# First-batch scans with one operand in PSUM, and a layer norm split between ScalarE and VectorE

## The chip, the cores and the metric

The kernel runs on one core of a Trainium2 chip. The metric is the device time of one execution in microseconds (us), lower is better; it is measured three times and the median is compared. The engines have short names here, as in the profile: PE is TensorE (its matmuls), PEld its weight loads, DVE is VectorE, ACT is ScalarE, POOL is GpSimd, and SP issues the transfers. Each engine takes its own instructions strictly in order and waits at an instruction whose inputs are not there, while whatever stands behind it waits too.

## The reference, cut to what matters

Three layers follow one another. The first is a recurrent attention with a decay for each key channel, the second a gated block with a layer norm, the third a gated convolution:

```python
state = np.zeros((B, H, D, D))                          # B = 4, H = 8, D = 48, S = 768
for t in range(S):
    cur = einsum('bhd,bhe->bhde', u * kt, vt)
    y[:, :, t] = einsum('bhd,bhde->bhe', rt, state + cur)
    state = wt[..., None] * state + einsum('bhd,bhe->bhde', kt, vt)

h = gelu(x @ w_in)                                      # x is y with the heads side by side
u, v = h[..., :512], h[..., 512:]
v_n = (v - mean(v)) / sqrt(var(v) + 1e-6) * g_ln        # the layer norm
gated = u * (einsum('ts,bsd->btd', w_sg, v_n) + b_sg)
x = x + gated @ w_out

gate = sigmoid(causal_conv5(x))
return (gate * (x @ w_val)) @ w_out2
```

## The kernel before

The attention is cut into 48 units: 4 batches, 3 segments of 256 tokens, 4 pairs of heads. Inside a unit the recurrence is done in 4 chunks of 64 tokens. `suffix` (step F, L270) multiplies the decays from the end of each chunk backwards by one scan on DVE; `prefix` (step E, L275) does it forwards. A scan is one instruction in which each column needs the result of the column before it; it reads two operands, `data0` and `data1`. For F and E the first is the decays `w` out of the loaded packet `pk`, and the second is a row of zeros with one entry for each chunk, where the product starts anew: `D1F` for F, `D1E` for E, both in SBUF. `r_part` and `k_part` (L, K) scale the queries and keys on POOL, `turn` (t) transposes the keys on PE, `scores` (s) and `causal` (m) make the masked products inside a chunk, and `kv` (B, L323) makes the sum of key-value products of each chunk in PSUM tile `a1`. `kv_out` (d, L346) copies them on ACT into the SBUF tile `SD1`, whose column 1 of every 6 holds the state that `keep` (p) carried over from the segment before. `states` (a, L350) then runs the third scan over 288 columns, `SD1` with `SD0` (the decays of whole chunks, put there by `chunk_decay`, D, on ACT), in place. `s_part` (S) copies the states on ACT, `tokens` (C, L366) makes the outputs on PE in another PSUM tile, `a2`, and `y_out` (y) adds them to `y` on DVE. In the first batch odd units have their PSUM tiles in another pool (`c0`, `c1`, `c2`).

In the first batch `warm` (L319) puts 3 extra bf16 matmuls of 256 columns ahead of `kv` and 2 ahead of `tokens`; their results are never read. Before, they are written into the tile that the real matmuls use afterwards, so they wait until that tile is free. 16 wider ones stand at the start of the program (L703, tile `wps`).

After the attention come, for each 128 tokens, a transpose (`xT`, L482 on DVE), `hv` (L490 and on: the matmul with the v half of `w_in`, gelu, layer norm and a split of the result in a high and a low part, so that three fp32r matmuls give an fp32 product), and for each half batch `u_step`, `vs_step` (the product with `w_sg`, tile `vps`), `gated`, `wo_step`, `conv`, `val_step`, `out_step`. Weights arrive as 64-bit numbers and are turned into fp32 by one ACT and four DVE instructions each (`to_f32`, L150 to L157), then split on ACT and POOL (L163, L164). The steps of batch b+1's attention are interleaved with the later layers of batch b by hand-written lists (`ORDER0`, `ORDER`, `LAST`), and within these a list scheduler with a priority table (`LEAD`) orders each engine's instructions by its own model of time.

Of the kernel before, what the change touches and what calls it, by code (L numbers as in the profile page):

```python
# [52 lines left out]
def tile_kernel(ctx, tc, pk, sv_, rk_, v_, u_, misc_, w_in, w_sgT, b_sg, w_o1, w_val,  # L53
# [193 lines left out]
    def unit(n):  # L247
# [22 lines left out]
        def suffix():  # L270
            dve.tensor_tensor_scan(out=F[:, NW:0:-1], data0=w[:, NW:0:-1], data1=D1F[:, NW:0:-1],  # L271
                                   initial=0.0, op0=ALU.mult, op1=ALU.add)
            dve.reciprocal(out=d1e[:, 0:NW:W1], in_=F[:, 1:NW + 1:W1])

        def prefix():  # L275
            dve.tensor_tensor_scan(out=E, data0=w[:, 0:NW], data1=d1e, initial=0.0,
                                   op0=ALU.mult, op1=ALU.add)
# [41 lines left out]
        def warm(o, k):  # L319
            for _ in range(k if first else 0):  # L320
                pe.matmul(out=o[:, 256:512], lhsT=wsrc[:, 0:128], rhs=wsrc[:, 0:256], start=True, stop=True)

        def kv():  # L323
            t["b"] = ps(1, n, [128, 512])
            warm(t["b"], WB)
            for j in range(NT):
                for hh in range(2):
                    pe.matmul(out=t["b"][half[hh], 2 * j * D:(2 * j + 2) * D],  # L328
                              lhsT=kn[:, j * 128 + 64 * hh:j * 128 + 64 * hh + 64],
                              rhs=vcd[:, j, :, hh * D:(hh + 1) * D], start=True, stop=True)  # L330
            if summed:
                for j in range(NT):
                    pe.matmul(out=t["b"][:, NC * D + 2 * j:NC * D + 2 * j + 2],
                              lhsT=q[:, j * 128:(j + 1) * 128], rhs=u_col[:, 2 * p:2 * p + 2], start=True, stop=True)

        def own_v():
            rs = r2.tile([128, 2 * NT], F32, tag="rsw", name="rsw")
            act.activation(out=rs, in_=t["b"][:, NC * D:NC * D + 2 * NT], func=AF.Copy)
# [49 lines left out]

# [450 lines left out]
```

## Time and profile before

| | us |
|---|---|
| median of 3 runs (lowest, highest) | 556.61 (556.54, 557.25) |
| the profiled execution | 556.39 |
| span of its instructions in the trace | 554.3 |
| PE / DVE / ACT / POOL busy in that span | 520.3 / 417.0 / 296.2 / 267.5 |

The span runs from the first instruction to the last; 2.1 us of the profiled execution lie around it. Busy time is the union of an engine's instructions. [...]

### The profile page before, as it was taken

The numbers are of one execution on the slowest core, as the hardware profiler recorded it, in microseconds if no ns is written. First come the engines' busy times: TensorE is split into PE (matmuls) and PEld (weight loads), VectorE is DVE, ScalarE is ACT, GpSimd is POOL, SyncE is SP. The second block draws the span as 40 slices with busy tenths as digits, with TensorE's granted clock in tenths as the row PEclk, the third lists the DMA queues.
The fourth block names the chain that finished last, engine by engine and source line by source line (L and its number), as shares of the span: only waits on it lengthen the run. The fifth ranks groups of instructions, "written<-read, shape, count | busy, mean of one in ns | idle before, by whom it ended". The sixth has DMA issues, their size and how long they took to land.

```text
span 554.3 us, 10705 instructions
## 1 busy us (share of the span) xinstructions
PE 520.3 (94%) x4060; PEld 448.4 (81%) x4060; DVE 417.0 (75%) x823; ACT 296.2 (53%) x695; POOL 267.5 (48%) x282
## 2 busy tenths in 40 slices
PE   8978688979999999898999999999999999999995
PEld 4666566868988887787988888789989887999985
DVE  6999999899697769985299669965498349324673
ACT  4676856655475745743285746643484636323233
POOL 7477856674844246764154126861163125523430
PEclk9598788896999999999999999999999999999999
DMA  8961513424314343342115342232122100100002
GB/s 302 388 246 44 164 66 103 133 83 158 86 43 138 108 144 100 100 128 90 41 38 178 124 122 72 59 121 80 44 54 91 58 16 1 43 1 0 1 0 86
DMA packets 27075, 53.42 MB, mean 96 GB/s; under 512 B 3089, under 2 KB 17169, under 8 KB 27025
## 3 DMA queue, kind: packets, MB, share of 16 engines
q1 hardware_dynamic: 27024, 52.75, 29.4%
q8 instruction: 32, 0.52, 0.4%
q14 instruction: 19, 0.15, 0.1%
HBM read 48.02 MB, written 4.72 MB: 95 GB/s over the span
## 4 chain that ended last, share of the span: by engine, by line
PE 40%; DVE 16%; issue 3%; DMA 2%; POOL 1%; ACT 1%; POOLq 0%; SPq 0%; ACTq 0%; DVEq 0%
PE vps L522 12%; PE c L586 6%; PE ups L522 6%; PE o L644 4%; DVE cvp L618 4%; PE val L522 3%; PE a L372 3%; PE hv L499 2%; PE a L303 2%; PE a L328 2%; DVE cv L618 1%; PE a L297 1%; DVE SD L353 1%; DVE rk L229 1%; DMA rk<-in_rk_dram 1%
## 5 line engine op out<-in xcount | busy, mean ns | idle before, releaser
L522 PE MATMUL vps<-wsg,vnt 128*128 128x384 f32 x576 | 113.1, 341 | 0.0
L522 PEld LDWEIGHTS vps<-wsg,vnt 128*128 128x128 f32 x576 | 101.1, 190 | 1.0
L573 POOL TENSOR_TENSOR gt<-gt,ut 128x384 f32<-128x384 f32 x32 | 33.8, 1057 | 98.7 <-DVE gt L562 80.5
L499 PE MATMUL hv<-win,x 128*128 128x512 f32 x216 | 65.2, 431 | 3.7 <-DVE cv L631 2.2
L586 PE MATMUL c<-gl,late 128*128 128x384 f32 x288 | 62.6, 345 | 0.0
L522 PE MATMUL ups<-x,win 128*128 128x384 f32 x288 | 59.8, 350 | 1.5 <-DVE gt L562 1.5
L358 ACT ACTIVATE SE<-SD 64x192 f32<-64x192 f32 x80 | 45.1, 564 | 23.1 <-DVE SD L353 13.9
L522 PEld LDWEIGHTS ups<-x,win 128*128 128x128 f32 x288 | 51.4, 192 | 3.0 <-DVE gt L562 1.9
L586 PEld LDWEIGHTS c<-gl,late 128*128 128x128 f32 x288 | 50.2, 189 | 2.2
L499 PEld LDWEIGHTS hv<-win,x 128*128 128x128 f32 x216 | 41.4, 202 | 12.8 <-DVE cv L631 2.6
L280 POOL TENSOR_TENSOR L<-pk,E 128x256 f32<-128x256 f32 x38 | 30.9, 814 | 41.1 <-PE a L372 32.9
L618 DVE SCALAR_TENSOR_TENSOR cvp<-x,cw_col,cvp 128x384 f32<-128x384 f32 x84 | 48.7, 612 | 0.4 <-ACT cvp L615 0.2
L271 DVE TENSOR_TENSOR_SCAN F<-pk,D1F 128x260 f32<-128x260 f32 x40 | 35.3, 884 | 16.5 <-DMA pk<-in_pk_dram 12.3
L353 DVE TENSOR_TENSOR_SCAN SD<-SD,SD 128x288 f32<-128x288 f32 x48 | 43.4, 903 | 4.6 <-ACT SD L347 4.2
L522 PE MATMUL val<-x2hl,late 128*128 128x384 f32 x216 | 44.2, 344 | 2.2 <-ACT vg L503 1.8
L644 PE MATMUL o<-late,ml 128*128 128x384 f32 x216 | 43.9, 342 | 0.7 <-DVE ml L634 0.7
L316 ACT ACTIVATE vcd<-v 64x192 f32<-64x192 f32 x84 | 30.2, 359 | 26.8 <-PE a L328 25.8
L515 POOL TENSOR_TENSOR vnt<-vg,vnt 128x512 fp32r<-128x512 f32 x24 | 34.2, 1426 | 17.9 <-ACT vnt L514 15.3
L576 DVE TENSOR_TENSOR gl<-gt,gl 128x384 fp32r<-128x384 f32 x32 | 20.0, 624 | 29.9 <-ACT gl L575 29.7
L522 PEld LDWEIGHTS val<-x2hl,late 128*128 128x128 f32 x216 | 37.3, 188 | 5.3 <-ACT vg L503 2.7
L575 ACT ACTIVATE gl<-gt 128x384 fp32r<-128x384 f32 x32 | 16.7, 523 | 42.9 <-POOL gt L573 38.2
L644 PEld LDWEIGHTS o<-late,ml 128*128 128x128 f32 x216 | 37.5, 187 | 2.4 <-DVE ml L634 1.0
(154 smaller groups left out, 1102.8 us busy)
## 6 DMA issues: line engine op xcount, KB each, us to landing
pk<-in_pk_dram SPq DMA_DIRECT2D x40, 386.5 KB, 3.4
sv<-in_sv_dram SPq DMA_DIRECT2D x39, 192.0 KB, 2.4
v<-in_v_dram SPq DMA_DIRECT2D x12, 384.0 KB, 3.3
out_dram<-ot SPq DMA_DIRECT2D x24, 192.0 KB, 1.9
rk<-in_rk_dram SPq DMA_DIRECT2D x12, 384.0 KB, 3.1
bits<-in_w_in_dram SPq DMA_DIRECT2D x6, 512.0 KB, 6.8
room_l<-in_pk_dram SPq DMA_DIRECT2D x7, 386.5 KB, 7.1
bits<-in_w_o_dram SPq DMA_DIRECT2D x7, 384.0 KB, 5.3
```

Source lines behind the costliest of these rows:

```text
L271: dve.tensor_tensor_scan(out=F[:, NW:0:-1], data0=w[:, NW:0:-1], data1=D1F[:, NW:0:-1], initial=0.0, op0=ALU.mult, op1=ALU.add)
L280: pool.tensor_tensor(out=ch(L[:, 0, :]), in0=ch(r), in1=e3[:, :, 0:C], op=ALU.mult)
L316: act.activation(out=vcd[half[c2], :, c2, :], in_=vt[b, s][half[c2], :, 2 * p * D:(2 * p + 2) * D], func=AF.Copy)
L353: dve.tensor_tensor_scan(out=SD1, data0=SD1, data1=SD0, initial=0.0, op0=ALU.add, op1=ALU.mult)
L358: act.activation(out=S[half[hh], :, hh, :], func=AF.Copy, in_=d1[half[hh], :, 1:NC + 1].rearrange("p e c -> p c e"))
L499: pe.matmul(out=ps, lhsT=x[:, a, kk, j * 128:(j + 1) * 128], rhs=win[:, w, kk, DV:2 * DV], start=(z == 0), stop=(z == nmm - 1))
L515: pool.tensor_tensor(out=vnt[b][:, 1, i, :], in0=vg, in1=hi.bitcast(F32), op=ALU.subtract)]
L522: pe.matmul(out=ps, lhsT=lhs(a, kk), rhs=rhs(w, kk), start=(z == 0), stop=(z == nk * 3 - 1))
L573: pool.tensor_tensor(out=t, in0=t, in1=ut.pop((b, hf, d)), op=ALU.mult)
L586: pe.matmul(out=acc[0][f], lhsT=late["wo1"][:, a, d, f * 128:(f + 1) * 128], rhs=g[:, w, :], start=(d == 0 and q == 0), stop=(d == KV - 1 ...
L618: dve.scalar_tensor_tensor(out=t, in0=x2[:, f, k:k + HALF], scalar=cw_col[:, f, k:k + 1], in1=t, op0=ALU.mult, op1=ALU.add)
L644: pe.matmul(out=acc2[0][j], lhsT=m[:, a, j * 128:(j + 1) * 128], rhs=late["wo2"][:, w, g, :], start=(g == 0 and q == 0), stop=(g == KD - 1 ...
```

## The change

There are two edits in one.

In the first batch all three scans get one operand in PSUM. A PSUM tile `D1` (a whole bank, the one that was `a2`) holds the start entries of both F and E. `kv` writes its products with a stride of 6 columns straight to where the third scan reads them, so the copy `kv_out` goes; the carried state comes into the same tile by an ACT copy of two columns of every 6 (a DVE memset in the first segment), and `keep` goes. `tokens` writes into the rest of the same bank, which is therefore held until `y_out`. The extra matmuls no longer write to the tile of the real ones but to `wps`, which is kept for that.

The layer norm's `(v - mean) * rstd` was one DVE instruction. Now ACT makes `mean - v` and the high part (`* rstd` on the way), and DVE makes the low part in one instruction with two SBUF inputs, which was POOL's. The sign is put right by a negated `g_ln` (`g_neg`).

```diff
-        F, E, d1e = buf("F", n), buf("E", n), buf("D1E", n)
+        F, E = buf("F", n), buf("E", n)
+        d1e, d1f = (D1, D1[:, D1F0:]) if first else (buf("D1E", n), D1F)
+        kvs = lambda: t["b"][:, 0:SDN].rearrange("p (e c) -> p e c", c=NC + 2)
+        KV0 = SDN + TOK if first else NC * D
...
-            dve.tensor_tensor_scan(out=F[:, NW:0:-1], data0=w[:, NW:0:-1], data1=D1F[:, NW:0:-1],
+            dve.tensor_tensor_scan(out=F[:, NW:0:-1], data0=w[:, NW:0:-1], data1=d1f[:, NW:0:-1],
...
-        def warm(o, k):
+        def warm(k):
             for _ in range(k if first else 0):
-                pe.matmul(out=o[:, 256:512], lhsT=wsrc[:, 0:128], rhs=wsrc[:, 0:256], start=True, stop=True)
+                pe.matmul(out=wps[:, 0:256], lhsT=wsrc[:, 0:128], rhs=wsrc[:, 0:256], start=True, stop=True)
...
-                    pe.matmul(out=t["b"][half[hh], 2 * j * D:(2 * j + 2) * D],
-                              lhsT=kn[:, j * 128 + 64 * hh:j * 128 + 64 * hh + 64],
+                    o = (kvs()[half[hh], :, 2 + 2 * j:4 + 2 * j].rearrange("p e c -> p c e") if first
+                         else t["b"][half[hh], 2 * j * D:(2 * j + 2) * D])
+                    pe.matmul(out=o, lhsT=kn[:, j * 128 + 64 * hh:j * 128 + 64 * hh + 64],
                               rhs=vcd[:, j, :, hh * D:(hh + 1) * D], start=True, stop=True)
...
         def kv_out():
+            if first:
+
+                if s == 0:
+                    dve.memset(kvs()[:, :, 0:2], 0.0)
+                else:
+                    act.activation(out=kvs()[:, :, 0:2], in_=d1[:, :, NC:NC + 2], func=AF.Copy)
+                return
             act.activation(out=d1[:, :, 2:NC + 2], func=AF.Copy,
...
-            dve.tensor_tensor_scan(out=SD1, data0=SD1, data1=SD0, initial=0.0,
+            dve.tensor_tensor_scan(out=SD1, data0=t["b"][:, 0:SDN] if first else SD1, data1=SD0, initial=0.0,
                                    op0=ALU.add, op1=ALU.mult)
...
-            if s < NSEG - 1:
+            if s < NSEG - 1 and not first:
                 act.activation(out=d1[:, :, 1], in_=d1[:, :, NC + 1], func=AF.Copy)
...
-            t["c"] = ps(2, n, [128, 512])
-            warm(t["c"], WC)
+            t["c"] = t["b"][:, SDN:SDN + TOK] if first else ps(2, n, [128, 512])[:, 0:TOK]
+            warm(WC)
...
-            ln = dve.tensor_scalar(out=vg, in0=vg, scalar1=mv[:, 0:1], scalar2=rs,
-                                   op0=ALU.subtract, op1=ALU.mult)
+
+            ln = act.activation(out=vg, in_=vg, func=AF.Identity, scale=-1.0, bias=mv[:, 0:1])
             hi = vnt[b][:, 0, i, :]
-            last[b * KS + i] = [ln, act.activation(out=hi, in_=vg, func=AF.Copy),
-                       pool.tensor_tensor(out=vnt[b][:, 1, i, :], in0=vg, in1=hi.bitcast(F32),
-                                          op=ALU.subtract)]
+            last[b * KS + i] = [ln, act.activation(out=hi, in_=vg, func=AF.Copy, scale=rs),
+                       dve.scalar_tensor_tensor(out=vnt[b][:, 1, i, :], in0=vg, scalar=rs,
+                                                in1=hi.bitcast(F32), op0=ALU.mult, op1=ALU.subtract)]
...
+    dve.memset(D1, 0.0)
+    dve.memset(D1[:, D1F0 + W1:D1F0 + NW + 1:W1], 1.0)
...
-    wps = psD.tile([128, 512], F32, tag="d", name="wps")
+    wps = psC.tile([128, 512], F32, tag="c2", name="wps")
```

The scheduler orders the instructions anew. On PE, at the start of the program, the kernel before has ten of the narrow extra matmuls (L321, into the tiles of the real ones) behind the 16 wide ones, and then the transposes and products of units 0 and 1. These rows run from the last extra matmul to the first unit's products (`a_204` and `a_224` are PSUM tiles of unit 0, `a_241` and `a_279` of unit 1, `kh` the scaled keys, `kn` their transpose):

```order
L321 LDWEIGHTS D1F
L321 MATMUL a_279<-D1F 128x256
L297 MATMUL a_204<-ident,kh_106 128x128 x2
L297 MATMUL a_241<-ident,kh_107 128x128 x2
L303 MATMUL a_204<-L_101,kh_106 64x64 x8
L328 MATMUL a_224<-vcd_119,kn_111 64x96 x4
L333 MATMUL a_224<-misc,pk_99 128x2 x2
```

In the changed kernel, on PE at the same place, eleven narrow extra matmuls stand ahead of the first transpose, one between the two transposes, and 21 behind them (the last pair of these rows is the first of the 21):

```order
L306 MATMUL a_208<-ident,kh_108 128x128 x2
L330 LDWEIGHTS D1F
L330 MATMUL wps<-D1F 128x256
L306 MATMUL a_245<-ident,kh_109 128x128 x2
L330 LDWEIGHTS D1F
L330 MATMUL wps<-D1F 128x256
```

So 33 extra matmuls now run ahead of the first unit's scores where ten did; 16 more stand between the transposes of units 2 and 3, 6 behind these, and the last of all 60 is issued ahead of unit 3's `kv`.

On DVE, the rows of the kernel before from the third unit's E scan to the second unit's masking (scans are listed here under the name SCALAR_TENSOR_TENSOR; L276 is the scan E, L271 F, L353 the scan over the states, L311 the masking, L291 the product of queries and keys):

```order
L276 SCALAR_TENSOR_TENSOR E_110<-room_l,D1E_112 128x260
L271 SCALAR_TENSOR_TENSOR F_109<-room_l,D1F 128x260
L291 TENSOR_TENSOR room_l<-room_l 128x256
L311 TENSOR_TENSOR L_101<-a_204,misc 128x256
L273 RECIPROCAL D1E_112<-F_109 128x4
L276 SCALAR_TENSOR_TENSOR room_w<-room_l,D1E_112 128x260
L353 SCALAR_TENSOR_TENSOR SD_115<-SD_115,SD_113 128x288
L311 TENSOR_TENSOR L_102<-a_241,misc 128x256
```

In the changed kernel, on DVE, the rows from the fourth unit's E scan on (L285 is that scan, `D_96` the PSUM tile `D1`, L157 to L163 the weights' conversion, L320 the masking, L360 the new memset in unit 0's PSUM tile):

```order
L285 SCALAR_TENSOR_TENSOR room_w<-room_l,D_96 128x260
L300 TENSOR_TENSOR room_l<-room_l 128x256
L157 TENSOR_SCALAR spare<-spare 128x512
L159 TENSOR_SCALAR spare<-spare 128x512
L161 SCALAR_TENSOR_TENSOR spare<-bits,spare 128x512
L157 TENSOR_SCALAR spare<-spare 128x512
L320 TENSOR_TENSOR L_103<-a_208,misc 128x256
L163 SCALAR_TENSOR_TENSOR spare<-bits,spare 128x512
L159 TENSOR_SCALAR spare<-spare 128x512
L360 MEMSET a_228 128x48x2
L320 TENSOR_TENSOR L_104<-a_245,misc 128x256
```

The maskings have moved behind all four units' F and E scans and behind four instructions of the weights' conversion, and the first scan over the states comes later still.

## Rows read from the trace of the kernel before

**Rows 1.** The page's head: span; busy time, share and instructions of the engines.

```profile
span 554.3 us, 10705 instructions
PE 520.3 (94%) x4060; PEld 448.4 (81%) x4060; DVE 417.0 (75%) x823; ACT 296.2 (53%) x695; POOL 267.5 (48%) x282
```

**Rows 2.** Windows: stretch, length, busy of each engine (instructions), granted clock, DMA share, GB/s.

```profile
10.00:74.70 64.70, 52.78 (x533) 39.77 (x534) 62.79 (x106) 44.54 (x116) 47.29 (x46) 0.78 0.59 212
...
84.20:141.00 56.80, 50.95 (x378) 42.61 (x378) 52.50 (x109) 32.91 (x80) 33.25 (x33) 0.85 0.38 118
141.00:520.00 379.00, 371.95 (x2890) 329.83 (x2889) 268.96 (x541) 198.48 (x457) 168.55 (x173) 1.00 0.25 76
```

**Rows 3.** Windows of L271 (scan F) alone, DVE, the first batch's twelve.

```profile
0.00:74.70 74.70, 11.79 (x12) 0.81 0.62 219
```

**Rows 4.** Windows of L276 (scan E) alone, DVE, the first batch's twelve.

```profile
0.00:74.70 74.70, 11.97 (x12) 0.81 0.62 219
```

**Rows 5.** Windows of L353 (scan over the states) alone, DVE, the first batch's twelve.

```profile
0.00:84.20 84.20, 10.85 (x12) 0.82 0.56 199
```

**Rows 6.** Instructions of one line: shortest/median/longest ns, first and last start (us).

```profile
L271 DVE TENSOR_TENSOR_SCAN F<-room_l,D1F x7: 668/700/1696, 9.8 to 64.5; 128x260 f32<-128x260 f32 x7
L276 DVE TENSOR_TENSOR_SCAN E<-room_l,D1E x4: 685/844/997, 10.8 to 49.6; 128x260 f32<-128x260 f32 x4
L353 DVE TENSOR_TENSOR_SCAN SD<-SD,SD x12: 717/945/1181, 14.7 to 83.1; 128x288 f32<-128x288 f32 x12
L311 DVE TENSOR_TENSOR L<-a,misc x42: 374/411/425, 13.1 to 441.4; 128x256 f32<-128x256 f32 x42
L283 DVE TENSOR_TENSOR kh<-pk,F x36: 390/426/1248, 75.6 to 427.1; 128x256 f32<-128x256 f32 x36
```

**Rows 7.** Timeline of DVE and POOL: start, duration (us), engine, line, operation.

```profile
3.83 0.70 DVE L271 TENSOR_TENSOR_SCAN F<-pk,D1F 128x260 f32<-128x260 f32 x1 [1.47 <-DMA pk<-in_pk_dram]
...
13.09 0.41 DVE L311 TENSOR_TENSOR L<-a,misc 128x256 f32<-128x256 f32 x1
...
30.27 1.70 DVE L271 TENSOR_TENSOR_SCAN F<-room_l,D1F 128x260 f32<-128x260 f32 x1
...
30.01 1.40 POOL L164 TENSOR_TENSOR win<-spare,win 128x512 fp32r<-128x512 f32 x1 [0.68 <-ACT win L163]
```

**Rows 8.** Timeline of PE: start, duration (us), line, operation.

```profile
7.02 1.04 PE L321 MATMUL a<-D1F 128*128 128x256 bf16 x8
...
9.92 0.68 PE L303 MATMUL a<-L,kh 64*64 64x64 f32 x16 [1.26 <-ACT kn L307]
10.53 0.55 PE L328 MATMUL a<-vcd,kn 128*64 128x96 f32 x8
```

**Rows 9.** Groups by line, whole span: count, busy us, mean ns, idle before.

```profile
L155 DVE SCALAR_TENSOR_TENSOR spare<-bits,spare 128x512 int32<-128x512 int32 x6 | 5.1, 848 | 0.1
L157 DVE SCALAR_TENSOR_TENSOR spare<-bits,spare 128x512 int32<-128x512 int32 x6 | 4.5, 743 | 0.0
L352 DVE MEMSET SD<- 128x48 f32 x16 | 1.6, 98 | 3.4 <-ACT SE L358 1.8 <-DMA pk<-in_pk_dram 1.0 <-POOL SD L697 0.7
L347 ACT ACTIVATE SD<-a 128x192 f32<-128x192 f32 x48 | 16.1, 336 | 6.0 <-PE a L328 3.2 <-PE a L333 2.0
L514 ACT ACTIVATE vnt<-vg 128x512 fp32r<-128x512 f32 x24 | 15.1, 630 | 28.7 <-DVE vg L511 26.6 <-DVE rstd L509 1.8 <-DVE x L544 0.2
L515 POOL TENSOR_TENSOR vnt<-vg,vnt 128x512 fp32r<-128x512 f32 x24 | 34.2, 1426 | 17.9 <-ACT vnt L514 15.3 <-DMA pk<-in_pk_dram 2.5
```

**Rows 10.** Windows of L511 (the layer norm's DVE instruction) alone, up to 141 us.

```profile
0.00:141.00 141.00, 4.44 (x6) 0.83 0.49 166
```

**Rows 11.** Windows of L321 (the extra matmuls) alone: PE, PEld, clock.

```profile
40.00:84.20 44.20, 5.11 (x25) 2.45 (x25) 0.81 0.27 86
```

**Rows 12.** Windows, all engines, columns as in group 2.

```profile
12.00:24.00 12.00, 11.16 (x97) 8.27 (x95) 10.54 (x22) 8.55 (x24) 6.82 (x8) 0.51 1.04 392
40.00:76.00 36.00, 27.91 (x249) 20.69 (x246) 35.69 (x61) 25.67 (x64) 28.45 (x27) 0.78 0.29 94
```

More of the change, by code (lines that the diff above doesn't have):

```diff
@@ L74, in tile_kernel @@
     u_bc = const.tile([128, DM], F32, name="u_bc")
+    g_neg = const.tile([128, KV], F32, name="g_neg")
     b_bc = const.tile([128, S], F32, name="b_bc")
@@ L78, in tile_kernel @@
     D1F = const.tile([128, NW + 1], F32, name="D1F")
+    D1 = psA.tile([128, 512], F32, tag="a2", name="D1")
+    D1F0 = NW - W1
     SDN = D * (NC + 2)
@@ L270, in suffix @@
         def suffix():
-            dve.tensor_tensor_scan(out=F[:, NW:0:-1], data0=w[:, NW:0:-1], data1=D1F[:, NW:0:-1],
+            dve.tensor_tensor_scan(out=F[:, NW:0:-1], data0=w[:, NW:0:-1], data1=d1f[:, NW:0:-1],
                                    initial=0.0, op0=ALU.mult, op1=ALU.add)
-            dve.reciprocal(out=d1e[:, 0:NW:W1], in_=F[:, 1:NW + 1:W1])
+            dve.reciprocal(out=d1e[:, 0:NW - C:W1], in_=F[:, 1:NW + 1:W1])
         def prefix():
-            dve.tensor_tensor_scan(out=E, data0=w[:, 0:NW], data1=d1e, initial=0.0,
+            dve.tensor_tensor_scan(out=E, data0=w[:, 0:NW], data1=d1e[:, 0:NW], initial=0.0,
                                    op0=ALU.mult, op1=ALU.add)
@@ L332, in kv @@
                 for j in range(NT):
-                    pe.matmul(out=t["b"][:, NC * D + 2 * j:NC * D + 2 * j + 2],
+                    pe.matmul(out=t["b"][:, KV0 + 2 * j:KV0 + 2 * j + 2],
                               lhsT=q[:, j * 128:(j + 1) * 128], rhs=u_col[:, 2 * p:2 * p + 2], start=True, stop=True)
@@ L337, in own_v @@
             rs = r2.tile([128, 2 * NT], F32, tag="rsw", name="rsw")
-            act.activation(out=rs, in_=t["b"][:, NC * D:NC * D + 2 * NT], func=AF.Copy)
+            act.activation(out=rs, in_=t["b"][:, KV0:KV0 + 2 * NT], func=AF.Copy)
             if p == 0:
@@ L350, in states @@
         def states():
-            if s == 0:
+            if s == 0 and not first:
                 dve.memset(d1[:, :, 1], 0.0)
-            dve.tensor_tensor_scan(out=SD1, data0=SD1, data1=SD0, initial=0.0,
+            dve.tensor_tensor_scan(out=SD1, data0=t["b"][:, 0:SDN] if first else SD1, data1=SD0, initial=0.0,
                                    op0=ALU.add, op1=ALU.mult)
@@ L376, in y_out @@
             y = yt[b, s][:, :, 2 * p * D:(2 * p + 2) * D]
-            dve.tensor_tensor(out=y, in0=t["c"][:, 0:NT * 2 * D].rearrange("p (j e) -> p j e", j=NT), in1=y, op=ALU.add)
+            dve.tensor_tensor(out=y, in0=t["c"].rearrange("p (j e) -> p j e", j=NT), in1=y, op=ALU.add)
         steps = {"F": suffix, "E": prefix, "L": r_part, "K": k_part, "D": chunk_decay, "q": ruk,
@@ L387, in tile_kernel @@
     STAGES = "FELKD", "tskmv", "BdaSp", "Cy"
+    TOK = NT * 2 * D
     def ps(i, n, shape):
@@ L561, in vs_step @@
         with lead("vso"):
-            dve.scalar_tensor_tensor(out=t, in0=ps, scalar=g_col[:, d:d + 1],
+            dve.scalar_tensor_tensor(out=t, in0=ps, scalar=g_neg[:, d:d + 1],
                                      in1=b_bc[:, hf * HALF:(hf + 1) * HALF], op0=ALU.mult, op1=ALU.add)
@@ L737, in tile_kernel @@
     late_weights()
+    act.activation(out=g_neg, in_=g_col, func=AF.Copy, scale=-1.0)
     ready = load_weights(rows(w_o1, KV), [XH, XH, XH, X2])
```

4 lines of the change are left out of this document (2 added, 2 removed).

## The prediction

> **What bounds the kernel now.** I read the page's head first, then the span cut into stretches, then single lines inside the stretch that matters. PE is busy 94% of the span [rows 1], which would make DVE look free. The stretches say otherwise [rows 2]. From 10.0 to 74.7 us DVE is busy 62.79 of 64.70 us and PE 52.78, at a mean granted clock of 0.78: this is the first batch's attention, and DVE ends it. From 84.2 to 141 us both are near their limit (DVE 52.50, PE 50.95 of 56.80). From 141 to 520 us PE is busy 371.95 of 379.00 us at full clock, with DVE at 268.96: there PE ends everything, and at most 7.05 us of idle PE could be won. So time that DVE saves before 74.7 us moves all that follows forward, while time saved on DVE or POOL after 141 us is nearly worthless.
>
> Where does DVE lose time in that first stretch? One line's shortest, median and longest instruction tell it [rows 6]. The scans have one shape each, yet F takes 668 to 1696 ns, E 685 to 997, the scan over the states 717 to 1181. The masking L311, of 256 columns with its first input in PSUM, takes 374 to 425 ns in all 42 cases; L283, of 256 columns with both inputs in SBUF, takes 390 at its shortest and up to 1248. The long F scan at 30.27 us begins while POOL is in an instruction from 30.01 to 31.41 us [rows 7]; what is left of POOL's instruction, 1.14 us, and an undisturbed scan of some 0.70 us give 1.84, and 1.70 was seen. I read it so: a DVE instruction with two SBUF inputs waits inside itself for POOL, one with an input in PSUM does not.
>
> **The change part by part.**
>
> *The scans.* The first batch's twelve F scans take 11.79 us [rows 3], the E scans 11.97 [rows 4], the twelve scans over the states 10.85 [rows 5]: 34.61 us. Undisturbed they would take 0.70 (F and E) and 0.73 us (states), which lie just above the shortest cases [rows 6]: 24 x 0.70 + 12 x 0.73 = 25.56. The gain is 9.05 us if PSUM as a source costs nothing of its own. No scan of this trace reads PSUM. The nearest pair is L311 (411 ns median from PSUM) against L283's shortest (390): no dearer by more than 21 ns, or by 35 ns with L311's longest, so that 36 scans lose 0.8 to 1.3 us at worst. On the other side no scan of 260 columns in these rows is shorter than 668 ns; at that, F and E would win 0.8 us more. I take 9.0, since the pair's rows are nearly equal, and keep 7.7 and 9.8 as the ends.
>
> [...]
>
> *What feeds the third scan.* Twelve ACT copies of 336 ns (L347, rows 9) go, and eight small copies of `keep` are replaced by eight of twice the columns. DVE gets four memsets of 96 strided columns: 48 columns take 98 ns [rows 9], so 0.10 to 0.20 each, 0.15 taken, +0.6 us. The four memsets that they replace ran at the very start, where DVE waits 1.47 us for the first packet [rows 7], and won nothing by going; the memsets of the new bank lie in that same wait, at no cost. The bank is held until `y_out`, so unit n+2's `kv` waits for unit n's last addition; by the tick's order this is issued a full tick earlier, and I cost it at nothing as long as DVE's queue, not this chain, sets the pace.
>
> *The extra matmuls.* 33 narrow ones now run ahead of the first scores in place of ten. Eight took 1.04 us [rows 8], 0.13 each, so the 21 behind the transposes take 2.7 us, and the first scores, at 9.92 us before [rows 8], come at about 12. What hides this is DVE's new order: its masking of unit 0, at 13.09 us before [rows 7], now stands behind the fourth unit's E scan and four instructions of the weights' conversion, work that has to be done anyway. Cost zero; 2 to 3 us if that cover is not there (the conversion waits for its own transfers).
>
> *The layer norm.* Up to 141 us DVE's six instructions of 4.44 us [rows 10] become six with two SBUF inputs of the kind of L155 and L157 (848 and 743 ns, rows 9): 4.5 to 5.1 us, +0.4 taken. ACT gets a pass of some 630 ns (L514, rows 9) for each, 3.8 us for the six, about what the twelve removed copies give back (4.0 us). POOL loses 24 instructions of 1426 ns, 34.2 us [rows 9]. In the first stretch that frees DVE's other instructions a little; I take nothing for it, up to 2 us. After 141 us the eighteen others shorten a chain that the vps matmuls do not wait on, beside a PE that is busy 98%: nothing taken, 2 us at most.
>
> **The sum**, against the profiled execution's own 556.39 us: -9.0 (scans) +0.6 (memsets) +0.4 (layer norm) = -8.0, so 548.4. The median of the runs stands 0.2 above that execution, hence 548.5 us.
>
> **The rivals.**
>
> *PE becomes the bound of the first batch (slower).* All 60 extra matmuls are now issued ahead of the fourth unit's `kv`; before, 25 of them ran between 40 and 84 us [rows 11]. After thin stretches the clock does fall: from 12 to 24 us it is 0.51, the lower level, behind PE's wait of 1.26 us ahead of the first scores [rows 8, 12]. From 40 to 76 us PE is busy 27.91 us at a mean clock of 0.78 [rows 12], of which the extra ones are about 5.11 x 36/44.2 = 4.2. If without them the clock stayed at 0.5 all through, the remaining 23.7 us would take 37.0, and with PE's 8.1 us of idle time 45.1 in place of 36. That is +9.1, against half of the scans' gain (4.5, an estimate by the share of units) won before 40 us: 561. It decides once PE with its gaps needs more than DVE's remaining 31 us there. Against it: with DVE faster, PE's real work comes denser, which is what the extra matmuls stood in for, and the early ones may spare the half-clock stretch at 12 us.
>
> *The gain is eaten (no change).* Either POOL's locks only move: the waits that left the scans turn up in the products and conversions that still have two SBUF inputs, and 9.0 shrinks towards 0. For it: from 40 to 76 us POOL is busy 28.45 of 36 us [rows 12]. Against it: scans that need no lock let POOL work beside them, and POOL is free sooner. Or the strided results of `kv` are slow: eight rows of one unit take 0.55 us [rows 8], so doubled, twelve units cost PE 6.6 us, of which its 11.9 us of idle in the first stretch [rows 2] hide most. Or the new order costs, in the tail behind 74.7 us, what was won: PE's idle there was kept small. Each leads to 553 to 557.5.
>
> [...] No run here shows a strided matmul result yet.
>
> *More is won.* POOL is relieved and its instructions shorten too, so that DVE's other two-input instructions lose their waits, and the half-clock stretch from 12 to 24 us, 11.16 us of busy PE [rows 12], runs faster: 3 to 8 us more, 540 to 545.
>
> **How the numbers follow.** Forecast (543.5 to 553): 0.55. More: 0.15. Eaten (553 to 557.5): 0.16. PE the bound (above 557.5): 0.14. The range 541 to 557 takes the forecast, most of the better case and nearly all of the case of no gain: 0.8. Within 0.2% of 556.61 us (555.5 to 557.7), about what a measurement of this kernel can tell from no change, lie 0.10, the middle of the third case; faster is 0.55 + 0.15 + 0.06 = 0.76, slower 0.14.
>
> **What would show it.** The 36 scans' lines with shortest and longest within some 60 ns of each other, F and E near 0.70, states near 0.73 to 0.78. DVE still busy 95% or more until batch 1 begins, which was at 74.7 us [rows 2] and should be near 67. PE's last long busy stretch the same length, moved forward by 8 us; L515 gone from POOL, the L535 low part on DVE at 0.75 to 0.85 us. It is wrong if the scans keep their spread, if the clock between 30 and 70 us falls under 0.7 with DVE idle, or if batch 1 starts earlier and the end does not follow.

## The result, and the profile after

The changed kernel is slower: 564.79 us (median of 4 runs, 563.61 to 565.99) against 556.58 us, ratio 1.014, 95% interval 1.0113 to 1.0167. The forecast was 548.5 us and a gain. Run again beside the experiments it took 565.25 us (ratio 1.0156, 1.0111 to 1.0201). The profiled execution took 565.74 us; its span is 564.0 us, 9.7 longer than before. (Of the experiments below, e3 alone ran anywhere from 551.0 to 563.8 us; its three quickest runs, which a ratio would rest on, give 0.9941, so its median and range are given instead.)

The page's head and three stretches of the windows of the changed kernel, which answer to [rows 1, 2]:

```profile
span 564.0 us, 10769 instructions
...
PE 520.1 (92%) x4060; PEld 451.0 (80%) x4060; DVE 401.4 (71%) x825; ACT 311.3 (55%) x708; POOL 226.9 (40%) x258
```

```profile
10.00:74.70 64.70, 51.84 (x538) 41.48 (x538) 56.89 (x116) 43.02 (x100) 37.75 (x43) 0.71 0.60 211
...
84.20:141.00 56.80, 49.80 (x366) 41.52 (x364) 45.84 (x96) 32.27 (x76) 24.96 (x27) 0.85 0.29 95
141.00:520.00 379.00, 365.81 (x2873) 322.55 (x2873) 260.76 (x538) 212.35 (x482) 142.67 (x153) 1.00 0.26 79
```

The engines got their savings: DVE is busy 15.6 us less than before and POOL 40.6 less. But DVE, busy 62.79 us of the first stretch before, is now busy only 56.89: what it saved turned into waiting, and batch 1's first scan starts at 74.4 us, where 67 was forecast. PE has as much busy time as before and 9.7 us more of idle time.

The scans by line (shortest, median, longest ns; first and last start), and the new low part of the layer norm, answer to [rows 6]:

```profile
L280 DVE TENSOR_TENSOR_SCAN F<-room_l,D x7: 664/677/696, 9.5 to 65.5; 128x260 f32<-128x260 f32 x7
L285 DVE TENSOR_TENSOR_SCAN E<-room_l,D x4: 675/691/697, 10.5 to 62.6; 128x260 f32<-128x260 f32 x4
L370 DVE TENSOR_TENSOR_SCAN SD<-a,SD x12: 723/745/757, 18.5 to 91.2; 128x288 f32<-128x288 f32 x12
L535 DVE SCALAR_TENSOR_TENSOR vnt<-vg,rstd,vnt x24: 719/752/1586, 58.8 to 487.9; 128x512 fp32r<-128x512 f32 x24
```

So the scans do what the change wants: none is stretched any more, and an operand in PSUM costs nothing that shows (F and E have medians of 677 and 691 ns; their shortest from SBUF in [rows 6] are 668 and 685). The loss is elsewhere. Windows of the stretches 0 to 28, 28 to 76 and 76 to 112 us, all engines, show where: first the kernel before,

```profile
0.00:28.00 28.00, 24.57 (x197) 16.62 (x197) 22.48 (x46) 15.36 (x41) 17.27 (x33) 0.76 0.96 346
28.00:76.00 48.00, 36.92 (x372) 27.71 (x371) 47.66 (x80) 34.71 (x88) 37.43 (x36) 0.83 0.40 139
76.00:112.00 36.00, 34.34 (x307) 25.73 (x306) 33.96 (x79) 22.93 (x57) 20.13 (x20) 0.89 0.36 112
```

then the changed kernel:

```profile
0.00:28.00 28.00, 23.51 (x226) 16.50 (x226) 23.00 (x50) 14.89 (x33) 19.22 (x35) 0.94 0.95 339
28.00:76.00 48.00, 37.71 (x359) 30.17 (x356) 40.60 (x83) 33.85 (x80) 26.02 (x32) 0.63 0.43 143
76.00:112.00 36.00, 28.51 (x217) 21.69 (x216) 26.03 (x57) 20.52 (x49) 12.07 (x15) 0.73 0.31 97
```

From 28 to 76 us the granted clock has fallen from 0.83 to 0.63 (such a figure is a mean: of 200 windows of 0.5 us from 10 to 110 us of the changed kernel, 113 show 0.50 and 79 show 1.00) and DVE has 7.4 us of idle time where it had 0.3; from 76 to 112 us PE gets 217 instructions done where it did 307. The extra matmuls alone (L330) in the windows of the changed kernel, which answer to [rows 11]:

```profile
0.00:28.00 28.00, 9.30 (x60) 6.48 (x60) 0.94 0.95 339
28.00:76.00 48.00, 0.00 (x0) 0.00 (x0) 0.63 0.43 143
```

All 60 run ahead of 28 us. In the kernel before, the same view has 26 of them there, 32 in 28 to 76 us and 4 behind (one that crosses an edge is in both rows, so these add up to 62).

Up to 28 us the units are late too: the first unit's third scan runs at 18.53 us, behind the weights' conversion on DVE, where it ran at 14.65 us before. By itself that is not the loss, for e2 below starts the same scan at 20.06 us and ends at the time of the kernel before.

How time is lost behind 28 us, on PE in the changed kernel's timeline (start, duration, operation, idle time before it):

```profile
52.75 0.55 PE L339 MATMUL a<-room_w 128*64 128x96 f32 x8 [0.97 <-DVE y L394]
...
58.28 0.60 PE L389 MATMUL a<-SE,L 128*64 128x96 f32 x4 [4.27 <-ACT SE L375]
...
63.68 0.59 PE L389 MATMUL a<-room_s,L 128*64 128x96 f32 x4 [2.74 <-ACT room_s L375]
...
66.08 0.91 PE L339 MATMUL a<-vcd,room_w 128*64 128x96 f32 x8
```

and on ACT at the same place:

```profile
55.73 0.72 ACT L534 ACTIVATE vnt<-vg,rstd 128x512 fp32r<-128x512 f32 x1
56.36 0.71 ACT L532 ACTIVATE vg<-vg,mv 128x512 f32<-128x512 f32 x1
56.97 0.23 ACT L362 ACTIVATE a<-SD 128x96 f32<-128x96 f32 x1
57.14 1.09 ACT L375 ACTIVATE SE<-SD 64x192 f32<-64x192 f32 x2
```

The scan that L375 copies ran on DVE from 54.32 to 55.04 us. The copy starts only at 57.14, behind the layer norm's two passes and the carry, and PE waits 4.27 us for it. Eight rows of `kv` take 0.55 us ahead of the gap, at a clock of 1.00, and 0.91 behind it, at 0.50. The gap can hardly be why the clock falls, though: in the windows it is 1.00 for the gap's first 0.3 us and 0.50 for all the rest of it.

```profile
48.00:54.30 6.30, 5.04 (x64) 3.83 (x62) 6.30 (x16) 5.34 (x14) 3.80 (x4) 1.00 0.00 0
54.01:54.31 0.30, 0.00 (x1) 0.00 (x0) 0.30 (x1) 0.30 (x1) 0.30 (x1) 1.00 0.00 0
54.31:58.28 3.97, 0.00 (x0) 0.00 (x0) 3.90 (x7) 3.90 (x10) 3.97 (x5) 0.50 0.85 297
```

The clock is at 0.5 from 56 to 76 us throughout, as it is from 32 to 44, of which this is one row of the windows by 4 us,

```profile
36.00:40.00 4.00, 4.00 (x37) 2.98 (x33) 2.65 (x6) 2.07 (x7) 4.00 (x6) 0.50 0.77 258
```

and once more from 92 to 108 us.

DVE also comes to wait for the loads of the next packets. In its waits up to 160 us the changed kernel has

```profile
DVE F L280 <- DMA pk<-in_pk_dram: 6.0, 4, 2.2
```

(us in total, times, longest), where the kernel before has 1.5 us in one and e9 below 2.1 in one. No run here moves these loads alone, so how much of the loss comes through them is open.

**A ledger of PE.** The windows by 4 us, summed over the span, give three numbers that add up to it: PE's idle time (length less busy), what it lost to the lower clock (an estimate: busy times 1 less the granted clock, which takes PE at 0.50 as half as fast; the eight rows of `kv` above took 1.65 times as long there), and the rest, which is its work at full clock. Before: 34.0 + 20.4 + 499.9 = 554.3 us. Changed: 44.0 + 25.2 + 494.9 (rounded) = 564.0. So the 9.7 us are +10.0 idle, +4.8 clock and -5.0 work. The work is the same but for the extra matmuls: back to back they overlap and cover 9.30 us where L321 covered 12.06 in the same 112 us; the rest of that term is not traced. From 28 to 112 us alone idle and clock cost 17.8 + 22.0 us where they cost 12.7 + 9.4; ahead of 28 us the clock gives 4.9 back, and 4.5 in 112 to 160 us, where the kernel before has its own half-clock stretch.

### The profile page after: what moved, and what is told of

Same layout as the page of the kernel before. It is cut to its first block, busy times and chain, and to the rows that moved or that the text cites. A ratio compares the mean times of both kernels' runs of the same rounds, so it can differ in the third digit from the quotient of the medians.

```text
span 564.0 us, 10769 instructions
## 1 busy us (share of the span) xinstructions
PE 520.1 (92%) x4060; PEld 451.0 (80%) x4060; DVE 401.4 (71%) x825; ACT 311.3 (55%) x708; POOL 226.9 (40%) x258
## 4 chain that ended last, share of the span: by engine, by line
PE 48%; DVE 26%; DMA 6%; issue 6%; ACT 3%; POOL 2%; SPq 0%; POOLq 0%; DVEq 0%; ACTq 0%
PE vps L542 14%; PE c L606 7%; PE ups L542 5%; PE o L664 4%; PE val L542 4%; DVE cvp L638 4%; PE a L389 3%; DMA pk<-in_pk_dram 3%; PE hv L519 3%; PE a L339 3%; PE a L312 2%; DVE SD L370 2%; DVE F L280 2%; DVE bs L525 2%; DVE vnt L535 1%
## 5 line engine op out<-in xcount | busy, mean ns | idle before, releaser
L542 PE MATMUL vps<-wsg,vnt 128*128 128x384 f32 x576 | 111.0, 339 | 0.0
L375 ACT ACTIVATE SE<-SD 64x192 f32<-64x192 f32 x80 | 44.9, 561 | 21.6 <-DVE SD L370 15.1
L542 PEld LDWEIGHTS ups<-x,win 128*128 128x128 f32 x288 | 50.1, 188 | 5.8 <-DVE gt L582 3.8
L519 PEld LDWEIGHTS hv<-win,x 128*128 128x128 f32 x216 | 42.4, 205 | 14.9 <-ACT x L501 2.7
L664 PE MATMUL o<-late,ml 128*128 128x384 f32 x216 | 45.1, 344 | 0.8 <-DVE ml L654 0.7
L280 DVE TENSOR_TENSOR_SCAN F<-pk,D1F 128x260 f32<-128x260 f32 x36 | 29.4, 816 | 22.3 <-DMA pk<-in_pk_dram 15.8
L542 PEld LDWEIGHTS val<-x2hl,late 128*128 128x128 f32 x216 | 37.3, 188 | 3.5 <-DVE cv L651 1.3
L619 POOL TENSOR_TENSOR x2hl<-x,x2hl 128x384 fp32r<-128x384 f32 x24 | 24.9, 1049 | 36.0 <-ACT x2hl L618 36.0
L370 DVE TENSOR_TENSOR_SCAN SD<-SD,SD 128x288 f32<-128x288 f32 x36 | 32.0, 888 | 8.1 <-ACT SD L364 7.9
```

Source lines behind the costliest of these rows:

```text
L370: dve.tensor_tensor_scan(out=SD1, data0=t["b"][:, 0:SDN] if first else SD1, data1=SD0, initial=0.0, op0=ALU.add, op1=ALU.mult)
L375: act.activation(out=S[half[hh], :, hh, :], func=AF.Copy, in_=d1[half[hh], :, 1:NC + 1].rearrange("p e c -> p c e"))
L519: pe.matmul(out=ps, lhsT=x[:, a, kk, j * 128:(j + 1) * 128], rhs=win[:, w, kk, DV:2 * DV], start=(z == 0), stop=(z == nmm - 1))
L542: pe.matmul(out=ps, lhsT=lhs(a, kk), rhs=rhs(w, kk), start=(z == 0), stop=(z == nk * 3 - 1))
L619: pool.tensor_tensor(out=hl[:, 1, f, :], in0=xx, in1=hl[:, 0, f, :].bitcast(F32), op=ALU.subtract)
L664: pe.matmul(out=acc2[0][j], lhsT=m[:, a, j * 128:(j + 1) * 128], rhs=late["wo2"][:, w, g, :], start=(g == 0 and q == 0), stop=(g == KD - 1 ...
```

## The experiments

Each was timed beside the kernel before on the same chip (medians of 557.0 to 558.4 us there). The ledger is that of the one profiled execution, so it fits the median only roughly: in e3, e8 and e15 that execution lies 3 to 7 us above the median, in e4, e6 and e9 some 2.5 us below it. e8 turned out to have the same order as the kernel before, and its ledger differs from that one's by 1.9 us of idle time and 4.8 of clock; differences of that size in the table tell nothing.

| | us | ratio (95%) | idle | clock | work |
|---|---|---|---|---|---|
| e1 layer norm alone | 557.83 | 1.0011 (0.9979 to 1.0042) | 35.9 | 18.2 | 501.8 |
| e2 scans alone | 558.50 | 1.0026 (1.0000 to 1.0052) | 39.1 | 20.9 | 495.8 |
| e3 extra matmuls in the real tiles | 559.58 | 551.0 to 563.8 us | 39.7 | 23.5 | 497.3 |
| e4 same, tokens in an own bank | 558.46 | 1.0021 (0.9992 to 1.0049) | 38.3 | 20.5 | 495.3 |
| e5 the change again | 565.25 | 1.0156 (1.0111 to 1.0201) | 44.5 | 22.8 | 495.9 |
| e6 as e4, no layer-norm part | 557.03 | 0.9991 (0.9965 to 1.0017) | 35.3 | 18.7 | 498.7 |
| e7 before, short scans | 555.13 | 0.9956 (0.9927 to 0.9984) | 34.7 | 18.5 | 501.2 |
| e8 before, one number of `LEAD` moved | 557.76 | 1.0009 (0.9980 to 1.0039) | 35.9 | 25.2 | 500.0 |
| e9 change, extra matmuls bound | 554.88 | 0.9943 (0.9908 to 0.9978) | 36.6 | 14.6 | 499.5 |
| e10 change, difference on DVE | 561.24 | 1.0057 (1.0021 to 1.0093) | 41.6 | 21.1 | 494.7 |
| e11 before, no extra matmuls | 564.17 | 1.0116 (1.0058 to 1.0174) | 47.6 | 20.8 | 493.6 |
| e12 e6 with more of them | 557.17 | 0.9972 (0.9936 to 1.0007) | 36.7 | 15.2 | 504.7 |
| e13 before, extra matmuls bound | 560.97 | 1.0085 (1.0053 to 1.0117) | 42.4 | 15.2 | 501.6 |
| e14 change, no extra matmuls | 555.97 | 0.9975 (0.9952 to 0.9997) | 42.3 | 24.7 | 488.0 |
| e15 e9, no layer-norm part | 555.89 | 0.9987 (0.9964 to 1.0010) | 37.3 | 25.5 | 498.0 |
| e16 e9 with 84 of them | 542.31 | 0.9757 (0.9716 to 0.9797) | 30.9 | 7.9 | 501.0 |
| e17 before with 84 of them | 566.77 | 1.0168 (1.0126 to 1.0209) | 41.6 | 23.2 | 500.0 |
| e18 e16, no layer-norm part | 560.55 | 1.0052 (1.0026 to 1.0078) | 37.1 | 17.8 | 504.1 |

**Which part costs?** Four theories: the extra matmuls' early end (clock), the bank held until `y_out`, the layer norm's passes in ACT's queue, or a mere reordering (the scheduler works out every engine's order anew from each edit). e1 is the kernel before with the layer-norm lines of the change; e2 the changed kernel with those lines as they were. e3 and e4:

```diff
-                pe.matmul(out=wps[:, 0:256], lhsT=wsrc[:, 0:128], rhs=wsrc[:, 0:256], start=True, stop=True)
+                pe.matmul(out=o, lhsT=wsrc[:, 0:128], rhs=wsrc[:, 0:TOK], start=True, stop=True)
-            warm(WB)
+            warm(t["b"][:, SDN:SDN + TOK], WB)
-            warm(WC)
+            warm(t["c"], WC)
...
-            t["c"] = t["b"][:, SDN:SDN + TOK] if first else ps(2, n, [128, 512])[:, 0:TOK]
+            t["c"] = ps(2, n, [128, 512])[:, 0:TOK]
```

(the last pair in e4 alone; 4 and 3 narrower matmuls in place of 3 and 2; not shown: `wps` goes back to its former pool in both, as it does in e6, e12 and e14, and in e4 all of the first batch's `tokens` take their bank from one pool).

> The kernel before with the layer norm's new split alone (difference and high part on ScalarE, low part on VectorE); the scans and the banks stay as they were. If the split is what loses (ScalarE's two passes stand ahead of the units' copies in its queue, VectorE gets a pass that waits for ScalarE): 562 to 565 us. If the loss comes from the banks and the extra matmuls of the first batch, this is near the kernel before: 554 to 558, with the granted clock of 10 to 74.7 us near 0.78. If it is only that every change of the order costs, 558 to 563.

> The changed kernel with the layer norm as it was before: the scans read PSUM, the states and the tokens share a bank, the extra matmuls go to a tile of their own. If the split is what loses: 547 to 550 us. If the shared bank or the early end of the extra matmuls loses: 562 to 567, the clock of 32 to 44 and 56 to 76 us again 0.5. [...]

> The changed kernel, but the extra matmuls write the tiles of their own unit again (192 columns instead of 256, so four and three instead of three and two in a unit), so they are spread over the first batch as before. If the early end of the extra matmuls loses (clock 0.5 in 32 to 44 and 56 to 76 us): the clock of 10 to 74.7 us comes back from 0.71 to 0.78 or more, and the time to 548 to 553 us. If the bank that is held until y_out loses, the clock may rise and the time stays at 561 to 566, PE still waiting for VectorE's y_out ahead of a unit's kv. If ScalarE's queue loses: 561 to 566 as well, VectorE's state scans still starting late behind ScalarE's copies.

> As the run with the extra matmuls in their unit's tiles, and the tokens get a bank of their own again, so that a unit's kv bank is free after the state scan and not only after y_out. If the held bank loses: 547 to 552 us, where the run without this edit stays above 560. If the extra matmuls' place alone loses, both runs are within 2 us of each other at 548 to 553. If neither, both stay at 561 to 566.

Each half alone costs nothing or 0.3%, and each repair takes 5 to 7 us off: no theory wins by itself (e2, e3 and e4 lie outside what each of their theories expected), and no median gets below the kernel before. e3's runs lie far apart: 551.0 us at a mean clock of 0.981, 563.8 at 0.952.

**Does VectorE's time move the end, and is reordering enough?** e5 is the change again, e6 is e4 without the layer-norm lines, e8 has one number of `LEAD` moved. e7 lets ten of the first batch's units run their F and E scans over 65 of the 260 columns:

```diff
+        f0 = NW - W1 if b == 0 and n > 1 else 0
+        e1 = W1 if b == 0 and n > 1 else NW
...
-            dve.tensor_tensor_scan(out=F[:, NW:0:-1], data0=w[:, NW:0:-1], data1=D1F[:, NW:0:-1],
+            dve.tensor_tensor_scan(out=F[:, NW:f0:-1], data0=w[:, NW:f0:-1], data1=D1F[:, NW:f0:-1],
...
-            dve.tensor_tensor_scan(out=E, data0=w[:, 0:NW], data1=d1e, initial=0.0,
+            dve.tensor_tensor_scan(out=E[:, 0:e1], data0=w[:, 0:e1], data1=d1e[:, 0:e1], initial=0.0,
```

> The changed kernel once more, beside the others of this set. If the two halves of the change (1.001 and 1.003 alone) really cost more together than apart: 562 to 566 us, ratio 1.010 to 1.017. If the first four runs fell badly: 557 to 560.

> The changed kernel without its layer-norm part, with the extra matmuls in their unit's tiles and the tokens in a bank of their own: of the change only the scans' operand in PSUM is left. It adds up the two repairs, of which each alone took some 6 us off the changed kernel. If they add: 550 to 553 us. If VectorE's time in the first batch was never what the end waits for, there is nothing to win behind the repairs: 555 to 558, ratio 0.997 to 1.003.

> The kernel before, with ten of the first batch's twelve units running their F and E scans over a quarter of the elements (65 of 260); values are wrong from there, the work that hangs on them is the same. It takes some 14 us off VectorE ahead of 75 us and moves no bank, no copy and no extra matmul. If time saved on VectorE there moves the end, as the prediction had it: 543 to 549 us. If TensorE's own work, its gaps and its clock set the end: 553 to 558, and TensorE's busy time at 141 to 520 us is as before.

> The kernel before with one number of the order's table moved by three (bon 100 to 103) and nothing else: how much a mere reordering is worth. If the order's fine grain costs as much as the change did: off by 4 us or more either way. If not: 555 to 558 us.

e7 decides the prediction's first step. In its windows the F and E scans up to 74.7 us,

```profile
0.00:74.70 74.70, 6.70 (x14) 0.77 0.62 219
...
0.00:74.70 74.70, 8.14 (x13) 0.77 0.62 219
```

take 14.8 us, three of batch 1's among them, where 24 took 23.8 [rows 3, 4]: 9 us less, and nearly 11 for the first batch's own 24 (14 were expected; the short ones take 0.26 us at best and up to 1.35). The end moves by 2.4 us (ratio 0.9956). Part of the freed time lies idle on DVE: in e7's windows, answering to [rows 2],

```profile
10.00:74.70 64.70, 56.66 (x564) 44.07 (x565) 57.20 (x113) 46.83 (x120) 43.00 (x46) 0.74 0.59 212
141.00:520.00 379.00, 368.54 (x2872) 326.12 (x2869) 267.27 (x541) 197.21 (x459) 162.71 (x168) 1.00 0.24 75
```

DVE has 57.20 busy, as in the changed kernel, and the clock is 0.74 where it was 0.78. Part of it did reach PE, whose idle time from 28 to 112 us falls from 12.7 to 6.4 us; but ahead of 28 us its idle time is 3.6 us more, and the clock's cost from 28 to 112 us does not fall (13.7 for 9.4). Like every edit, e7's also gave a new order.

e8 tells nothing about reordering: its trace has the instructions of the kernel before in the same order on every engine, so it is that kernel once more. No run here changes the order alone. That eight runs whose orders differ from that of the kernel before (e1, e2, e4, e6, e7, e12, e14, e15) lie between 555 and 559 us speaks against reordering as the whole loss, but is no test of it. e6 shows nothing to win behind both repairs.

**The extra matmuls.** e9 edits nothing but what they read: each reads its unit's own data, so it cannot run earlier; what it writes is still read by nobody. e11 is the kernel before with `WB, WC = 0, 0`; e12 has six and four a unit in e6's version.

```diff
-                pe.matmul(out=wps[:, 0:256], lhsT=wsrc[:, 0:128], rhs=wsrc[:, 0:256], start=True, stop=True)
+                pe.matmul(out=wps[:, 0:256], lhsT=wsrc[:, 0:128], rhs=x.bitcast(mybir.dt.bfloat16)[:, 1:512:2], start=True, stop=True)
-            warm(WB)
+            warm(kn, WB)
-            warm(WC)
+            warm(buf("L", n)[:, SEG:2 * SEG], WC)
```

> The changed kernel, its 60 extra matmuls still 256 columns wide and still in a tile of their own, but each reads data of its own unit (kn ahead of kv, the masked scores ahead of the tokens; their output is read by nobody), so none can run before its unit has come that far. Only their place differs. If their early end is what costs: 556 to 560 us, and the clock of 28 to 44 us comes back from 0.5 to 0.6. If the place is not it: 563 to 566.

> The kernel before without its 60 extra matmuls (the 16 at the start stay). What they are worth where they stand. If their place matters as the theory has it: 561 to 567 us, the clock of 28 to 76 us at 0.5 to 0.6 where it was 0.8. If they are worth little: 555 to 559, and their early end in the changed kernel can't be what costs 8 us.

> The version with the scans' operand in PSUM alone (tokens in a bank of their own, no layer-norm part, 557.0 us), with six and four extra matmuls in a unit instead of four and three. Its clock is 0.5 at 12 to 24, 56 to 76 and 92 to 100 us, some 16 us of TensorE time more than at full clock. If the clock is what keeps VectorE's free time from showing: 549 to 554 us. If TensorE has no room for more columns: 557 to 561.

Here one condition of the loss shows: e9 takes 10 us off the changed kernel and is under the kernel before, and a little under its own expectation. Its windows, with those of L330 alone behind them,

```profile
28.00:76.00 48.00, 39.91 (x439) 30.18 (x438) 45.28 (x91) 36.59 (x88) 29.26 (x34) 0.86 0.42 140
76.00:112.00 36.00, 34.60 (x290) 26.97 (x287) 32.49 (x79) 27.71 (x67) 14.99 (x19) 0.91 0.43 133
...
28.00:76.00 48.00, 6.52 (x35) 3.06 (x35) 0.86 0.42 140
```

have the clock back at 0.86 and 0.91, and DVE idle 2.7 us in place of 7.4 from 28 to 76 us. The order changed with the place, so the 10 us are those of both. On DVE the first unit's masking and third scan stand in the changed kernel and in e9 at

```profile
15.86 0.42 DVE L320 TENSOR_TENSOR L<-a,misc 128x256 f32<-128x256 f32 x1
18.53 0.75 DVE L370 TENSOR_TENSOR_SCAN SD<-a,SD 128x288 f32<-128x288 f32 x1
...
13.46 0.40 DVE L320 TENSOR_TENSOR L<-a,misc 128x256 f32<-128x256 f32 x1
15.31 0.74 DVE L370 TENSOR_TENSOR_SCAN SD<-a,SD 128x288 f32<-128x288 f32 x1
```

with eight instructions of the weights' conversion ahead of that scan in the changed kernel and one in e9. In the kernel before the 60 are worth 6 us (e11). e12 meets the second of its expectations: there was no time to win with more of them.

**The layer norm's share.** e10 gives the difference back to DVE:

```diff
-            ln = act.activation(out=vg, in_=vg, func=AF.Identity, scale=-1.0, bias=mv[:, 0:1])
+            ln = dve.tensor_scalar(out=vg, in0=vg, scalar1=mv[:, 0:1], scalar2=-1.0, op0=ALU.subtract, op1=ALU.mult)
```

> The changed kernel, but the layer norm's difference is again a VectorE pass (it waits for the mean alone, not for POOL's power), ScalarE keeps only the high part and VectorE the low part. One ScalarE pass less that heads its queue and waits for VectorE's mean, one VectorE pass more. If ScalarE's wait at that pass holds up the units' copies behind it: 557 to 560 us, ScalarE's idle time ahead of the pass (8.4 us in all) gone. If it is the place of the extra matmuls and the bank: 564 to 567.

It wins some 4 us (561.24 against 565.25 in e5) and lands between the two expectations: the pass has a share, not the whole. In the waits up to 141 us the changed kernel has

```profile
ACT vg L532 <- DVE mv L527: 8.4, 3, 4.1
```

(us in total, times, longest), which goes with the pass; in e9 that line reads 2.9 us in 2 times, in e16 0.7 in one, and in e1, the layer norm alone, 1.7 in 2. So the pass does not bring the wait by itself; that it grows where PE delivers `hv` late is an argument, not shown.

**Is the gain the change's, and where is the rest?** e13 binds the extra matmuls in the kernel before (same reading, same banks as ever); e14 is the change with `WB, WC = 0, 0` (and `wps` in its former pool); e15 is e9 without the layer-norm lines; e16 is e9 with `WB, WC = 4, 3`; e17 is the kernel before with 4 and 3; e18 is e16 without the layer-norm lines.

> The kernel before, its extra matmuls where they were, in their unit's banks, but each reading its unit's own data as in the run that put the changed kernel at 554.9 us. A control: if that reading alone makes the order better, this is at 553 to 555.5 too and the change itself gains nothing. If the gain of 3.5 us is the change's own: 556 to 560.

> The changed kernel without its 60 extra matmuls. If they do no good where they end up, all ahead of 26 us, there is nothing to lose: 562 to 567, within 3 us of the changed kernel. If they are still worth some 6 us as in the kernel before: 569 to 573.

> The scans' operand in PSUM with the extra matmuls bound to their unit, without the layer-norm part. How much of the 3.5 us is the scans', and whether the layer-norm part is a loss once the extra matmuls are back. If the layer-norm part is worth nothing or costs a little (1.001 alone): 552 to 556 us. [...]

> The changed kernel with the extra matmuls bound to their unit and four and three in a unit in place of three and two (84 in place of 60). If the clock ahead of 112 us (still 0.5 to 0.6 in 12 to 32, 52 to 68 and 84 to 92) is what is left of the missing gain: 549 to 553 us. If TensorE has no room left: 555 to 559.

> The kernel before with 84 extra matmuls in place of 60, in their unit's banks as ever. The control of the run at 542.3 us. If more extra matmuls are all that it takes: 544 to 550 us, the clock at 1.0 ahead of 76 us here too. If VectorE's freed time is needed to keep TensorE fed between them: 555 to 562.

> The run at 542.3 us without the layer-norm part: scans with an operand in PSUM, shared bank, 84 extra matmuls bound to their unit. If the gain is the scans' and the clock's: 541 to 547 us. If the layer-norm part is needed for it: 552 to 559.

e13 is slower than the kernel before by 0.85%, so the binding is no gain by itself, and what e9 gains takes the change. e14 was under every expectation: without any extra matmul the change takes 556.0 us, so the 60 where they ran cost 9 us and bought nothing (its ledger differs from the change's by 6.9 us of work, about what the 60 take, and 2.2 of idle and clock). e16 is the fastest version, 2.4% under the kernel before and well under its own expectations. Its windows:

```profile
0.00:28.00 28.00, 21.70 (x237) 14.51 (x237) 23.14 (x55) 16.97 (x40) 18.58 (x35) 1.00 0.95 343
28.00:76.00 48.00, 41.71 (x469) 31.56 (x468) 45.78 (x105) 38.55 (x92) 31.37 (x38) 1.00 0.48 158
76.00:112.00 36.00, 35.53 (x284) 28.99 (x283) 33.76 (x72) 26.19 (x63) 17.22 (x20) 0.81 0.39 124
```

The clock never falls before 76 us, DVE does 105 instructions in 28 to 76 us where it did 80, and of the 14.5 us between the spans 12.5 are clock and 3.1 idle. Neither part is enough: in the kernel before 84 extra matmuls lose 9.7 us (e17, beyond both expectations). One of PE's waits of 28 to 76 us is longer there, 7.0 us for 1.0 before,

```profile
PE a L321 <- DVE y L377: 7.0, 3, 4.0
```

an extra matmul heads PE's queue until `y_out` frees its tile. But PE's idle time in that stretch is 7.7 us in all, 11.1 before; it is larger ahead of 28 us (7.0 for 3.4) and from 76 to 112 (6.2 for 1.7), and why is not traced. And without the layer-norm part the same 84 take 560.6 us (e18, beyond its second expectation), with 9.9 us more clock, 6.2 idle and 3.1 work than e16. The difference is spread: 2.0 us up to 76 us, 5.1 in 76 to 112, where the windows have (e16's row above)

```profile
76.00:112.00 36.00, 30.36 (x231) 24.21 (x228) 32.10 (x68) 20.60 (x51) 21.47 (x24) 0.76 0.36 111
```

and 5.1 more idle and clock in 160 to 300 us. Which of the instructions that went back to POOL and DVE costs what, these runs don't tell. With 60 instead of 84 the layer-norm part makes no difference that can be told (e9 against e15), so its worth may hang on the state of the clock, and e16's 542.3 is one point found, not a rule of 84.

## Why the prediction was wrong, step by step

**"Time that DVE saves before 74.7 us moves all that follows forward": the step that failed first.** DVE was busy 97% there, but it waited in order beside a PE that lost 12.0 us to its clock and 14.5 to idling up to 76 us. The change took 9.2 us off the scans, and batch 1 began at 74.4 us where it had at 74.7; e7 took nearly 11 us off them and left banks and copies alone, and the end moved by 2.4. A busy share of 97% showed that DVE was full, not that the end waited for it; PE's idle and clock terms of that stretch are what a saving must lower, and they were not worked out.

**"Cost zero" for the extra matmuls: the step that turned the sign.** The cover that was named held: the first scores came at 11.8 us (about 12 was forecast) and DVE was busy 10.1 of the 10.5 us from 9.48 to 20. But the cost was looked for only there. What counted was that nothing bound them any more: 10 us between e9 and the change, by their place and the order that comes with it. Not their absence behind 28 us alone, though: without any of them the change takes 556.0 (e14), and with the same early end but the old layer norm 558.5 (e2). It takes the early end and the layer norm's passes together to lose 8 us, and why they add up so steeply stays open: that PE's gaps, the half clock and ACT's wait for late `hv` feed each other fits the traces, but no run shows it.

**The rival "PE becomes the bound" came nearest**, with the place, the fall of the clock and nearly the time (561 against 565), at a chance of 0.14. From 40 to 76 us the clock is 0.64, not the 0.5 of its sum, and its premise, that the extra matmuls are missing there, is not enough by e2 and e14; the nearness of the time is partly luck. Its two counterarguments were weighed too high: ahead of 28 us, with the early extra matmuls, the clock was higher (0.94 against 0.76 before, and 0.77 in e14 without any), worth 4.9 us, but PE's real work came no denser behind (17.8 us idle from 28 to 112 us, 12.7 before).

**The scans: right.** F 8.21, E 8.27, states 8.90 us, together 25.38 (forecast 25.56, before 34.61). No time added by a source in PSUM shows: F and E have medians of 677 and 691 ns, where 668 and 685 were the shortest from SBUF in [rows 6], and the states' shortest is 723 ns against 717 from SBUF.

**Memsets right** (0.14 us each, 0.15 forecast). **The held bank right**: PE's `kv` waited 2.1 us for `y_out` up to 100 us, and 3.7 in e9, which is faster. **The strided `kv` right**: with a stride of 6 columns in the result eight rows take 0.55 us, as they did without it [rows 8].

**The layer norm: sized a little low, placed wrong.** Up to 141 us DVE's six low parts (L535) and ACT's six new passes (L532) take

```profile
0.00:141.00 141.00, 5.74 (x6) 0.79 0.47 159
0.00:141.00 141.00, 4.33 (x6) 0.79 0.47 159
```

where 4.5 to 5.1 and 3.8 us were forecast; with the 4.44 of [rows 10] DVE pays 1.3 us more instead of 0.4. Besides, the sum left out that ACT's pass waits for DVE's mean with the units' copies behind it. Giving the pass back to DVE wins some 4 us in the changed kernel (e10), while alone, in the kernel before, the part costs nothing (e1).

Of the signs named beforehand, the scans' held. DVE was busy 88% in the first stretch, not 95%, batch 1 did not come forward, and "wrong if the clock between 30 and 70 us falls under 0.7 with DVE idle" came true (0.63, with 5.6 us idle).

## What to carry to other kernels

A saving on a full engine is worth what it takes off the idle and half-clock time of the engine that bounds the rest (in e7 nearly 11 us off DVE moved the end by 2.4): make that ledger by stretches first, and try the saving alone, as a shortened instruction, before building it. Work that only fills gaps ran here wherever its dependencies let it (all 60 ahead of 28 us), so look where it has gone whenever a tile changes, and try binding it to the step that it is to fill; that paid in the changed kernel (e9) and cost 0.85% in the kernel before (e13). When two edits that cost nothing apart cost 1.4% together, look for a condition that they share (here the fillers) before undoing the edits. And look into the built order: an edit that was meant to reorder may change nothing (e8), and one that was not may change it everywhere (e9).

## What was not expected of the hardware

A PE that counts as busy is not thereby fast: from 32 to 44 us of the changed kernel it is busy 12.0 of 12 us at 0.50, while in e16 it idles 6.3 of 48 us at 1.00. Nor does the gap of 4.27 us account for the clock's fall to 0.50, which came 0.3 us after it began. One kernel can also end on either side of this: e3's ten runs differ by 12.8 us, and its mean clock by 0.03; and e8's profiled execution, of the same order as the kernel before, is 6.8 us longer, 4.8 of it clock.
